# One loop of seven passes on TensorE, with two shared buffers and GpSimd handing out its waits

## The chip, the cores and the metric

The kernel runs on one core of one Trainium2 chip. The metric is the device time of one execution in microseconds (us). Before the change it is 265.19 us, the median of three runs (265.16 to 265.31). A core has five engines that run their own instruction streams and meet only at semaphores: TensorE (PE, with its weight loads listed apart as PEld), VectorE (DVE), ScalarE (ACT), GpSimd (POOL) and SyncE (SP). Here SP does nothing but start transfers from memory. Sixteen DMA engines carry them.

## The reference, cut to what matters

One decode step of a transformer block for 8 sequences: layer norm, attention over the last 1024 positions of a cache, residual, layer norm, gated feed-forward, residual. Everything is float32, and every weight is used once.

```python
W = min(4096, max(256, Sk // 4))                # 1024
q = (layernorm(x) @ wq)                         # 8 x 1024 by 1024 x 4096
scores = einsum(q, k_cache[:, :, Sk - W:]) * (Dh ** -0.5)
o = einsum(softmax(scores), v_cache[:, :, Sk - W:])
h = x + o @ wo                                  # 8 x 4096 by 4096 x 1024
g, u = layernorm(h) @ w_gate, layernorm(h) @ w_up   # 1024 x 3584 each
out = h + (gelu(g) * u) @ w_down                # 3584 x 1024
```

The operands are 16.8 MB each for wq, the keys, the values and wo, and 14.7 MB each for gate, up and down: 111.15 MB that must come from memory.

## The kernel before, in words

**Loads.** SP issues every large transfer in the order of use. There are two buffers of 64 KB a partition (8.39 MB each). `load` (L127) takes them in turn: wq in two halves, keys in two, values in two, wo in two, then gate and up for the first four blocks of 512 columns (`gu0_0`, `gu0_1`). A load waits on SP until PE has marked the last product of what the buffer held before (`free[wb]`). The gate and up of the remaining three blocks (48 KB a partition each), and `w_down` in six parts (`PARTS`, 8, 8, 4, 4, 2 and 1 row blocks of 128 rows) and a last block in two column halves (`ends`), are laid out as a ring over the same 128 KB (L413 to L453). So there is always one load in flight and one or more waiting behind it.

**Side loads.** Of row block 19 (`SIDE`) the last 296 columns do not come with their part. Eight small transfers of 4 rows (L440) bring them to a tile of their own, `w_side`, from which eight extra products are made (L476).

**Products.** The 8 tokens are repeated to 32 columns. Each product takes a 128 x 32 stationary tile and 512 columns of the buffer. Four of them write the four groups of 32 PSUM partitions. A load of 8.39 MB is 32 such products; each is two matmul instructions and two weight loads in the stream. Between loads PE transposes what VectorE has made of the last sums (L192), and VectorE or ScalarE copies it into the next stationary tile. Every product of the program is written out: the PE stream is straight-line code.

**The tail.** The pair of row blocks 24 and 25 (L466), a single block (L489), the sum of the four PSUM groups through `d1` (L480 and L489), and the two `ends` halves (L501), two copies to SBUF on ACT (L504) and two output transfers.

## Time and profile before

| what | value |
|---|---|
| median of three runs | 265.19 us |
| span of the profiled execution | 264.1 us |
| outside the span, so median less span | 1.1 us |
| moved by the DMA queues | 111.44 MB, 422 GB/s on the mean |
| PE busy | 142.2 us (54%) |
| DVE, ACT, POOL busy | 23.3, 10.9, 5.5 us |

A row of the timeline gives start, duration, engine, line, operation, `out<-in`, shapes and the count of merged instructions; in brackets stands the idle time before it and what ended that. `x64` for a load's products are the 32 products with two matmul instructions each. A row of the windows view gives a stretch, its length, the busy time of each engine in it, the granted TensorE clock, the mean busy share of the 16 DMA engines and the GB/s moved. In the list of DMA queues `q1` carries what SP issues, `q10` what ACT issues and `q8 instruction` the transfers that refill an engine's instruction memory.

### The profile page before, as it was taken

The numbers are of one execution on the slowest core, as the hardware profiler recorded it, in microseconds if no ns is written. First come the engines' busy times: TensorE is split into PE (matmuls) and PEld (weight loads), VectorE is DVE, ScalarE is ACT, GpSimd is POOL, SyncE is SP. The second block draws the span as 40 slices with busy tenths as digits, with TensorE's granted clock in tenths as the row PEclk, the third lists the DMA queues.
The fourth block names the chain that finished last, engine by engine and source line by source line (L and its number), as shares of the span: only waits on it lengthen the run. The fifth ranks groups of instructions, "written<-read, shape, count | busy, mean of one in ns | idle before, by whom it ended". The sixth has DMA issues, their size and how long they took to land.

```text
span 264.1 us, 2072 instructions
## 1 busy us (share of the span) xinstructions
PE 142.2 (54%) x958; PEld 40.9 (15%) x958; DVE 23.3 (9%) x55; ACT 10.9 (4%) x17; POOL 5.5 (2%) x15
## 2 busy tenths in 40 slices
PE   0006905905905906907807507818609477589875
PEld 0002201201201301302202102212102111113122
DVE  0040000000020110110110100170000200000001
ACT  1020000000010020020000000020000000000000
POOL 8000000000000000000000000000000000000000
PEclk9999985865875975985956965975957959599999
DMA  8998999999899989999998999899998999999994
GB/s 318 481 437 357 476 476 390 407 466 466 347 466 466 459 347 466 459 407 417 447 466 367 469 437 466 377 447 457 429 419 387 476 402 427 417 462 409 410 413 181
DMA packets 3256, 111.44 MB, mean 422 GB/s; under 512 B 392, under 2 KB 648, under 8 KB 1072
## 3 DMA queue, kind: packets, MB, share of 16 engines
q1 hardware_dynamic: 3088, 111.22, 97.9%
q8 instruction: 7, 0.11, 0.2%
q10 hardware_dynamic: 160, 0.10, 0.1%
q14 instruction: 1, 0.01, 0.0%
HBM read 111.18 MB, written 0.13 MB: 421 GB/s over the span
## 4 chain that ended last, share of the span: by engine, by line
DMA 78%; PE 21%; SPq 0%; issue 0%; ACT 0%
DMA w<-gu 20%; DMA w<-wq 16%; DMA w<-v 11%; DMA w<-kt 11%; DMA w<-wo 11%; DMA w<-dn 9%; PE big L380 6%; PE tb L312 4%; PE tb L237 4%; PE ya L340 3%; PE big L265 3%; SPq L91 0%; PE acc L489 0%; ACT o_fin L504 0%; PE tb L489 0%
## 5 line engine op out<-in xcount | busy, mean ns | idle before, releaser
L380 PE MATMUL big<-w,ln_t 128*32 128x512 f32 x224 | 37.7, 752 | 19.8 <-DMA w<-gu 19.8
L265 PE MATMUL big<-w,qz 128*32 128x512 f32 x128 | 18.8, 753 | 18.3 <-DMA w<-kt 18.3
L340 PE MATMUL ya<-w,ot 128*32 128x512 f32 x128 | 17.9, 721 | 19.9 <-DMA w<-wo 19.9
L466 PE MATMUL ya<-w,at 128*32 128x512 f32 (+1 forms) x104 | 16.4, 591 | 3.2 <-DMA w<-dn 3.2
L380 PEld LDWEIGHTS big<-w,ln_t 128*32 128x32 f32 x224 | 9.2, 134 | 46.9 <-issue 24.9
L192 PE MATMUL ta<-ident,ln_xn 64*128 64x64 f32 x16 | 2.2, 318 | 24.4 <-DVE ln_xn L218 24.4
L312 PE MATMUL tb<-w,pt 128*32 128x512 f32 x64 | 9.9, 787 | 9.0 <-DMA w<-v 9.0
L312 PE MATMUL acc<-w,pt 128*32 128x512 f32 x64 | 9.4, 751 | 9.5 <-DMA w<-v 9.5
L237 PE MATMUL tb<-w,ln_t 128*32 128x512 f32 x64 | 9.8, 783 | 8.6 <-DMA w<-wq 8.6
L237 PE MATMUL acc<-w,ln_t 128*32 128x512 f32 x64 | 9.2, 742 | 2.6 <-DMA w<-wq 2.6
L340 PEld LDWEIGHTS ya<-w,ot 128*32 128x32 f32 x128 | 4.8, 128 | 31.5 <-issue 31.5
L265 PEld LDWEIGHTS big<-w,qz 128*32 128x32 f32 x128 | 4.8, 134 | 31.6 <-issue 22.5
L466 PEld LDWEIGHTS ya<-w,at 128*32 128x32 f32 x104 | 4.2, 109 | 15.0 <-issue 10.6
L393 DVE TENSOR_TENSOR hm<-ge,big 128x512 f32<-128x512 f32 (+1 forms) x2 | 1.4, 684 | 56.6 <-PE big L380 56.6
L192 PEld LDWEIGHTS ta<-ident,ln_xn 64*128 64x128 f32 x16 | 1.8, 216 | 25.3 <-DVE ln_xn L218 25.3
L274 DVE TENSOR_REDUCE nmax<-big 128x1 f32<-128x1024 f32 x2 | 2.4, 1224 | 33.8 <-PE big L265 33.8
L276 ACT ACTIVATE p<-big,nmax 128x1024 f32<-128x1024 f32 x2 | 2.2, 1113 | 71.9 <-DVE nmax L274 71.9
L312 PEld LDWEIGHTS tb<-w,pt 128*32 128x32 f32 x64 | 2.6, 139 | 15.6 <-issue 15.6
L312 PEld LDWEIGHTS acc<-w,pt 128*32 128x32 f32 x64 | 2.5, 135 | 15.7 <-issue 15.7
L237 PEld LDWEIGHTS tb<-w,ln_t 128*32 128x32 f32 x64 | 2.3, 139 | 15.4 <-DMA w<-wq 8.8
L237 PEld LDWEIGHTS acc<-w,ln_t 128*32 128x32 f32 x64 | 2.5, 134 | 8.6 <-issue 8.6
L209 ACT ACTIVATE ln_sd<-ln_ve 64x1 f32<-64x1 f32 x2 | 0.4, 203 | 73.9 <-DVE ln_ve L208 73.9
(81 smaller groups left out, 53.1 us busy)
## 6 DMA issues: line engine op xcount, KB each, us to landing
w<-gu SPq DMA_DIRECT2D x2, 6144.0 KB, 23.9
w<-dn SPq DMA_DIRECT2D x2, 4096.0 KB, 27.0
w<-dn SPq DMA_DIRECT2D x1, 2048.0 KB, 19.6
w<-dn SPq DMA_DIRECT2D x1, 1900.0 KB, 23.3
w<-dn SPq DMA_DIRECT2D x1, 1024.0 KB, 21.7
w<-dn SPq DMA_DIRECT2D x1, 512.0 KB, 22.5
w<-ends SPq DMA_DIRECT2D x2, 256.0 KB, 22.7
w_side<-side SPq DMA_DIRECT2D x8, 18.5 KB
```

The source lines that it names most:

```text
L192: tok = run("tensor", lambda e, i=i: e.transpose(t[:, i, :], src[:, i * P:(i + 1) * P], ident[:rows, :rows]), id_ok, ready, clear, mark=(i ...
L209: tok = run("scalar", lambda e: e.activation(sd, ve, AF.Sqrt), tok)
L237: tok = run("tensor", lambda e, c=c, j=j: e.matmul(q_ps[32 * j:32 * j + 32, :], xt[c], w[:, c, j * N:(j + 1) * N], start=(c == 0), stop=(c ...
L265: tok = run("tensor", lambda e: e.matmul(s_ps[32 * r:32 * r + 32, k0:k0 + N], qz[hf][:, s, c0:c0 + 32], k_t[:, s, half * HB + b, k0:k0 + N ...
L274: tok = run("vector", lambda e: e.tensor_reduce(out=nmax, in_=s_ps, axis=AX.X, op=ALU.max, negate=True), tok)
L276: p_ok = run("scalar", lambda e: e.activation(p_sb, s_ps, AF.Exp, bias=nmax, accum_out=tot), tok)
L312: tok = run("tensor", lambda e: e.matmul(o3[32 * r:32 * r + 32], pt[:, c, 32 * r:32 * r + 32], v_t[:, s, c, half * HB:(half + 1) * HB, :], ...
L340: tok = run("tensor", lambda e: e.matmul(ya[32 * r:32 * r + 32, :], ot[:, 2 * hf * REP + h + e2].rearrange("p r b -> p (r b)"), w[:, h + e ...
L380: tok = run("tensor", lambda e: e.matmul(pair[32 * j:32 * j + 32, s, :], ht[c], w[:, c, j * N:(j + 1) * N], start=(c == 0), stop=(c == NC ...
L393: tok = run("vector", lambda e: e.tensor_mul(hm[:rows], ge[:rows], pair[:rows, 1, :]), tok, g_ok)
L466: tok = run("tensor", lambda e: e.matmul(ya[32 * r:32 * r + 32, 0:n], at[:, q + e2, :], rows_of(q + e2)[:, ch * N:ch * N + n], start=(r no ...
```

## The change

All products are brought to one form, and PE runs them in a loop.

* **Two buffers, two stationary tiles, two PSUM pairs.** `buf[0]`, `st[0]`, `ob[0]` serve the first half of a pass (`a`), `buf[1]`, `st[1]`, `ob[1]` the second (`b`). A half is 8 steps of 4 products; the first 4 steps sum in one PSUM bank, the last 4 in the other, so the two banks are added afterwards by VectorE. Passes 0 to 5 are q, scores, values, wo, gate and up (blocks 0 to 3), gate and up (blocks 4 to 6, with 8 early row blocks of `w_down` in the free quarter of the load). Pass 6 has a first half alone: 16 row blocks of `w_down`.
* **Loads.** 11 transfers of 8.39 MB (`w_k_s`), the twelfth in two halves, pass 6 in 4, 2 and 2 steps (`wd0` to `wd2`), then a pair (`wp`), a single (`ws`) and the two `ends`. The side loads are gone; the input `x` comes in one transfer and not in two.
* **Waits.** PE waits on one semaphore, `go`, each time for 1, and takes it down again. GpSimd, after its own constants, walks a list in PE's order, waits for whatever each place needs and raises `go`.
* **The loop.** `Fori` over 7 passes on PE alone, with a branch that skips the second half in the last pass and one that runs the residual's products (`fold`, `res`) in pass 3 alone. Each transposition takes 8 blocks of 128 x 128, whether 1, 4 or 8 are used.
* **Tail.** After the loop: pair, single, `d1`, ends as before, with `d1` now the sum of two banks and of `d0`, which holds the residual and the early rows' sums.

```diff
-SET = NQ * N
-PARTS = (8, 8, 4, 4, 2, 1)
-SIDE = 19
+STEPS = 8
+LOAD = STEPS * NQ * N
+PASSES = 7
+WO, GU0, GU1, DN = 3, 4, 5, 6
+CUTS = (0, 4, 6, STEPS)
...
+    landed = {(0, 0): [move("w_0_0", buf[0], w[0])]}
+    x_in = move("x", x_sb[0:ROWS:STEP, :], x, x_zero, engine="scalar")
+    landed[0, 1] = [move("w_0_1", buf[1], w[1])]
+    for k in range(1, DN):
+        for s in range(2):
+            n = 2 * k + s
+            free = pe(f"{'ab'[s]}{k - 1}")
+            if (k, s) == (GU1, 1):
+                half = LOAD // 2
+                landed[k, s] = [
+                    move(f"w_{k}_{s}_{i}", buf[s][:, i * half:(i + 1) * half], w[n + i], free)
+                    for i in range(2)]
+            else:
+                landed[k, s] = [move(f"w_{k}_{s}", buf[s], w[n], free)]
+    landed[DN, 0] = [
+        move(f"wd{i}", buf[0][:, a * NQ * N:b * NQ * N], dn[i], pe(f"a{GU1}"))
+        for i, (a, b) in enumerate(zip(CUTS, CUTS[1:]))]
+    w_pair = buf[1][:, 0:NQ * N]
+    pair_in = move("wp", w_pair, pair, pe(f"b{GU1}"))
...
+    def tokens_in(ready):
+        xt = t8[:, :, 0:ROWS].rearrange("p n (b s) -> p n b s", s=STEP)[:, :, :, 0]
+        a = run("vector", lambda e: e.tensor_copy(
+            st[0].rearrange("p (c r b) -> p c r b", c=NC, b=B),
+            xt.unsqueeze(2).to_broadcast([P, NC, P // B, B])), *ready)
+        b = run("scalar", lambda e: e.copy(st[1], st[0]), a)
+        return a, b
...
-            side_in = fl.sem("w_side")
-            for h, src in enumerate(side):
-                p0 = h % 4 + 32 * (h // 4)
-                fl.start("sync", lambda e: e.dma_start(w_side[p0:p0 + 13:4], src), [zero[-1]]).then_inc(
-                    side_in, 16)
...
+    tok = run("vector", lambda e: e.tensor_add(d1, ob[0][:, 0:N], d0), pe(f"a{DN}h"), d0_ok, ex_ok)
...
+    d1_ok = run("vector", lambda e: e.tensor_add(d1, ob[0][:, N:2 * N], d1), pair_done, tok)
...
+    for name in pe_waits():
+        left = fl.missing("gpsimd", need.pop(name, []))
+        for s, v in left[:-1]:
+            nc.gpsimd.wait_ge(s, v)
+        if left:
+            nc.gpsimd.wait_ge(*left[-1]).then_inc(go, 1)
+        else:
+            nc.gpsimd.sem_inc(go, 1)
...
+    def wait():
+        nc.tensor.wait_ge(go, 1).then_inc(go, -1)
...
+    def turn(src):
+        for i in range(NC):
+            ins = nc.tensor.transpose(t8[:, i, :], src[:, i * P:(i + 1) * P], ident)
+        marked(ins)
+
+    def products(s, cuts):
+        for i in range(STEPS):
+            if i in cuts:
+                wait()
+            for r in range(NQ):
+                c = i // (STEPS // 2) * N
+                ins = nc.tensor.matmul(
+                    ob[s][32 * r:32 * r + 32, c:c + N], st[s][:, i * P + 32 * r:i * P + 32 * r + 32],
+                    buf[s][:, (i * NQ + r) * N:(i * NQ + r + 1) * N],
+                    start=(i % (STEPS // 2) == 0), stop=(i % (STEPS // 2) == STEPS // 2 - 1))
+            if i % (STEPS // 2) == STEPS // 2 - 1:
+                marked(ins)
+
+    wait()
+    turn(xs[1])
+    with nc.Fori(0, PASSES, engines=[mybir.EngineType.PE]) as it:
+        products(0, CUTS)
+        with nc.tensor.If(it < DN):
+            wait()
+            turn(xs[0])
+            products(1, (0, STEPS // 2))
+            with nc.tensor.If(it == WO):
+                wait()
+                for ch in range(2):
+                    ins = nc.tensor.matmul(
+                        fin[0:ROWS, ch * N:(ch + 1) * N], to_rows[:, ch, :], y_sb, start=True, stop=True)
+                marked(ins)
...
+            wait()
+            turn(xs[1])
```

What this moves on PE, at the start of the program. Before, each stage has rows of its own (`ln_t`, `qz`, `pt` are the stationary tiles of q, scores and values):

```order
L192 MATMUL ta<-ident,ln_xn 128x64 x8
L237 MATMUL acc<-w,ln_t 32x512 x32
L192 MATMUL ta<-ident,q 128x128 x4
L237 MATMUL tb<-w,ln_t 32x512 x32
L192 MATMUL ta<-ident,q 128x128 x4
L265 MATMUL big<-w,qz 32x512 x64
L192 MATMUL ta<-ident,p 128x128 x4
L192 MATMUL ya<-ident,p 128x128 x4
L312 MATMUL acc<-w,pt 32x512 x32
```

After, one body stands for all stages; the branches are instructions of PE (behind these rows come the loop's counter and its branch back):

```order
L433 MATMUL tt<-ident,xs 128x128 x8
L451 UNCONDITIONAL_BRANCH
L442 MATMUL o<-w,st 32x512 x32
L453 COMPARE_AND_BRANCH
L433 MATMUL tt<-ident,xs 128x128 x8
L442 MATMUL o<-w,st 32x512 x32
L457 COMPARE_AND_BRANCH
L460 MATMUL fin<-y_sb,to_rows 64x512 x2
L465 MATMUL fin<-h_sb,spread 32x512 x2
L457 UNCONDITIONAL_BRANCH
L433 MATMUL tt<-ident,xs 128x128 x8
L453 UNCONDITIONAL_BRANCH
```

The products of six stages have become two rows of 32 that are run again and again, and after each of them stand 8 transpositions where there were 1, 4 or 8.

On SP, from the gate and up loads to the end, before:

```order
L91 DMA w<-gu 128x16384 x2
L91 DMA w<-gu 128x12288 x2
L91 DMA w<-dn 128x8192 x2
L440 DMA w_side<-side 4x1184 x8
L91 DMA w<-dn 128x3800
L91 DMA w<-dn 128x4096
L91 DMA w<-dn 128x2048
L91 DMA w<-dn 128x1024
L91 DMA w<-ends 128x512 x2
```

and the whole of SP's transfers after (`w<-ends` are all pieces that are cut from one array, from the twelfth load's halves on):

```order
L81 DMA w<-w 128x16384 x11
L81 DMA w<-ends 128x8192 x3
L81 DMA w<-ends 128x4096 x2
L81 DMA w<-ends 128x2048
L81 DMA w<-ends 128x1024
L81 DMA w<-ends 128x512 x2
L81 DMA out<-o_fin 128x128
```

The eight transfers of 4 rows have gone, every load now spans all 128 partitions, and the last four loads are of the same sizes as before.

## The prediction

> **What bounds the kernel now.** I read the page first, then PE's timeline, then the DMA list cut at the landings, then the windows at the end.

> ```profile
> span 264.1 us, 2072 instructions
> PE 142.2 (54%) x958; PEld 40.9 (15%) x958; DVE 23.3 (9%) x55; ACT 10.9 (4%) x17; POOL 5.5 (2%) x15
> q1 hardware_dynamic: 3088, 111.22, 97.9%
> q8 instruction: 7, 0.11, 0.2%
> DMA 78%; PE 21%; SPq 0%; issue 0%; ACT 0%
> ```

> The 16 DMA engines are busy 97.9% of the span with the kernel's own 111.2 MB, and the chain of waits is 78% transfers. PE's 21% there are products between a landing and the issue of the load that replaces it. PE's timeline shows that this costs the stream nothing; the loads' first products, in order:

> ```profile
> 23.17 9.22 PE L237 MATMUL acc<-w,ln_t 128*32 128x512 f32 x64 [2.64 <-DMA w<-wq]
> 42.43 9.83 PE L237 MATMUL tb<-w,ln_t 128*32 128x512 f32 x64 [8.57 <-DMA w<-wq]
> 62.56 10.01 PE L265 MATMUL big<-w,qz 128*32 128x512 f32 x64 [8.82 <-DMA w<-kt]
> 82.02 8.82 PE L265 MATMUL big<-w,qz 128*32 128x512 f32 x64 [9.45 <-DMA w<-kt]
> 101.40 9.36 PE L312 MATMUL acc<-w,pt 128*32 128x512 f32 x64 [9.54 <-DMA w<-v]
> 120.81 9.89 PE L312 MATMUL tb<-w,pt 128*32 128x512 f32 x64 [9.02 <-DMA w<-v]
> 140.21 8.74 PE L340 MATMUL ya<-w,ot 128*32 128x512 f32 x64 [9.25 <-DMA w<-wo]
> 159.84 9.16 PE L340 MATMUL ya<-w,ot 128*32 128x512 f32 x64 [10.64 <-DMA w<-wo]
> 179.19 9.72 PE L380 MATMUL big<-w,ln_t 128*32 128x512 f32 x64 [1.30 <-DMA w<-gu]
> 198.45 8.63 PE L380 MATMUL big<-w,ln_t 128*32 128x512 f32 x64 [9.55 <-DMA w<-gu]
> ```

> A load lands about every 19.4 us and PE is done with it after 9 to 10, so the next load for that buffer is queued more than 9 us before the DMA engines run out of work. Only the stream and what follows its last byte set the time.

> The periods are not equal. From the starts: 19.26, **20.13**, 19.46, 19.38, 19.41, 19.40, **19.63**, 19.35, 19.26. The DMA list, cut from 23.2 to 42.4 us and from 42.4 to 62.5, tells what is special in the long one:

> ```profile
> DMA packets 144, 8.39 MB, mean 437 GB/s; under 512 B 16, under 2 KB 16, under 8 KB 16
> DMA packets 145, 8.41 MB, mean 418 GB/s; under 512 B 16, under 2 KB 16, under 8 KB 16
> q8 instruction: 1, 0.02, 0.3%
> ```

> The long period has one packet more, 16 KB of PE's instructions (0.11 MB over 7). A load has landed only when the last of 16 engines is done, and one such packet made the last engine 0.75 us later (20.13 less the mean of the other seven normal periods, 19.36). The second long period, +0.27, holds one too (the same list from 140.1 to 159.7 counts one), and others fell in normal periods: they hit engines that were not the last. If all seven had hit one engine, the landings would have slid by 7 x 0.75 = 5.3 us; they slid by about 1. So each delayed another engine. The end shows the result:

> ```profile
> 258.60:259.20 0.60, 0.06 (x4) 0.06 (x8) 0.00 (x0) 0.00 (x0) 0.00 (x0) 1.00 0.97 382
> 259.20:259.80 0.60, 0.60 (x8) 0.09 (x8) 0.00 (x0) 0.00 (x0) 0.00 (x0) 1.00 0.68 263
> 259.80:260.40 0.60, 0.42 (x8) 0.02 (x4) 0.13 (x1) 0.00 (x0) 0.00 (x0) 1.00 0.72 277
> 260.40:261.00 0.60, 0.60 (x16) 0.35 (x16) 0.56 (x1) 0.00 (x0) 0.00 (x0) 1.00 0.32 123
> 261.00:261.70 0.70, 0.70 (x29) 0.65 (x29) 0.06 (x1) 0.00 (x0) 0.00 (x0) 1.00 0.01 3
> ```

> The DMA share (next to last column) falls over nearly 2 us: some engines are done at 259.2, others at 261. The mean engine ends at 259.2 + 0.6 x (0.68 + 0.72 + 0.32) = 260.2, 0.8 before the last.

> **The change part by part.**

> *The instruction stream (the main term).* The page counts 958 matmul instructions and 958 weight loads, 1916, and 7 refills: one for each 256 to 274 instructions. In the change the program text holds, by the rows of PE's order, 96 products and 24 transpositions, that is 96 x 2 + 24 = 216 matmul instructions, 432 with their weight loads: less than two refills' worth. The loop's body is 68 products and 16 transpositions, 304 instructions: more than one refill holds, less than two. If what is in instruction memory stays, the seven refills go. By the rate: the stream ran from the second landing (42.4) to the last. The row of the last pieces gives that one:

> ```profile
> L91 SPq DMA_DIRECT2D w<-ends x2: 431/432/432, 238.3 to 238.8; - x2
> DMA to landing us min/median/max: 22.6/22.7/22.8
> ```

> 238.8 + 22.8 = 261.6. In these 219.2 us came 111.15 - 16.78 = 94.4 MB. At a normal period's rate (8.39 MB in 19.36 us, 433 GB/s) they need 217.8: 1.4 us less. That is an upper bound, as the small pieces at the end may never reach the full rate. By the engines: 0.8 us of imbalance, plus the refills' own time, 0.2% of 264.1 = 0.5 us an engine, less the imbalance that stays because the engines don't start together. I can't read the latter off a row; between 0 and 0.8 the gain is 0.5 to 1.3. Between 0.5 and 1.4 I take **1.1**: two normal neighbours, 19.26 and 19.46, differ by 0.2, so the engines' order at the start seems to matter little.

> *Side loads removed.* Eight times 18.5 KB go and w_down's part grows from 1900 KB to 2048: the same bytes, spread over all engines instead of shifted to some. **0** (in the 1.1, which assumes an even spread).

> *The form of the loads.* 8.39 MB as before, and the last four pieces have the same sizes as before. **0.**

> *More work between passes.* All transpositions are now 8 of 128 x 128, the stationary tile is 128 x 1024, and each sum has two banks to add.

> ```profile
> L192 PE MATMUL ta<-ident,q 128*128 128x128 f32 x8 | 1.3, 286 | 1.6 <-DVE q L243 1.6
> L223 DVE COPY ln_t<-ta 128x256 f32<-128x256 f32 x2 | 0.8, 424 | 2.4 <-PE ta L192 2.4
> L354 DVE TENSOR_TENSOR h_sb<-x_sb,big 64x1024 f32<-64x1024 f32 x1 | 1.2, 1214 | 2.2 <-PE big L351 2.2
> L393 DVE TENSOR_TENSOR hm<-ge,big 128x512 f32<-128x512 f32 x1 | 0.7, 686 | 28.9 <-PE big L380 28.9
> ```

> Eight transpositions took 1.3 us, four of them half: +0.65. An extra sum is +0.7, a copy to 128 x 1024 about 1.2 instead of 0.4. So a change of pass grows by 2 to 3 us, under covers of 8.6 to 9.6 us of idle PE (the brackets above). The one thin cover is 1.30 us, at 179.19, where residual and layer norm stand ahead of gate and up. There the additions are the copy (+0.8), transpositions (1.3 against 1.1) and the hand-overs: up to 1.5 us, so PE may start 0.2 late. Late next is the issue of the load that reuses the buffer, and it has over 9 us. **0.** Without that cover it would cost 2 to 3 us in each of 12 halves.

> *GpSimd between PE and what it waits for.* No row has this hand-over. Behind GpSimd's waiting instruction are only later waits in PE's order. The nearest is a hand-over from ACT to DVE in the layer norm:

> ```profile
> 17.52 0.20 ACT L209 ACTIVATE ln_sd<-ln_ve 64x1 f32<-64x1 f32 x1 [12.70 <-DVE ln_ve L208]
> 17.76 0.15 DVE L210 RECIPROCAL ln_r<-ln_sd 64x1 f32<-64x1 f32 x1 [0.27 <-ACT ln_sd L209]
> ```

> ACT ended at 17.72, DVE began at 17.76: a hop is under 0.1. There are now two hops instead of one; bounds 0 and 0.3 a wait. All are under the same covers but for the last, `wd2`'s, and the pieces behind it are waited for by PE itself:

> ```profile
> 256.64 1.92 PE L466 MATMUL ya<-w,at 128*32 128x512 f32 x16 [0.93 <-DMA w<-dn]
> 259.14 1.07 PE L466 MATMUL ya<-w,at 128*32 128x512 f32 x8 [0.57 <-DMA w<-dn]
> 260.38 0.43 PE L489 MATMUL acc<-w,at 128*32 128x128 f32 x8 [0.17 <-DMA w<-dn]
> 261.70 0.40 PE L501 MATMUL tb<-w,at 128*32 128x128 f32 x8
> 261.95 0.27 ACT L504 COPY o_fin<-acc 128x128 f32<-128x128 f32 x1 [22.45 <-PE acc L501]
> ```

> 0.57 us of idle PE covers it. **0**, at most 0.3.

> *The tail.* After the pair (landed 259.1): 4 products, one VectorE instruction of 0.7, eight small products, the ends, ACT, the transfer out. The same instructions in the same order; `d1` is an addition instead of a copy (686 against 691 ns). It moves with the landings. The loop's two branches stand ahead of the pair under the same 0.57 us. **0**, bounds 0 and 0.5.

> Sum: 264.1 - 1.1 = 263.0 of span; with the 1.1 us around it, or from the median, 265.2 - 1.1 = **264.1 us**.

> [...]

> **The rivals.**

> 1. *The loop refetches in every pass (slower).* Place: the branch back, from the body's second piece to its first. For it: PE took a refill at each piece of straight code, and the body needs two pieces. Against: nothing in the trace shows a piece dropped that is still wanted. PE's own stall would lie under the 9 us covers; the price is the engines'. One refill delays an engine by at least 0.75 and, by the width of the end, at most 1.8; I take 1.5. It decides from the point where some engine is hit twice, the 17th refill at the latest. With 13 refills (first piece back, next piece ahead) on different engines, all end about 1.5 late: 264.1 + 1.5 = 265.6, no change. With three a pass, 19, some engines are hit twice: 264.1 + 3 = 267.1 at most. All on one engine would be 10 us, which the slide in the trace speaks against.

> 2. *One to three refills remain (no change).* The second piece has to come in once. For it: the first refill in the trace came at the first piece's end. One engine is 1.5 late: 264.1 + 0.4 to 1.5, centre 264.9.

> 3. *The tail takes it back.* The pair's products wait for the loop's exit longer than 0.57 us: 264.1 + 0.5 to 1.

> 4. *PE is late for a buffer.* It would need 9 us more in a half; ruled out to a few per cent.

> **How the numbers follow.** About 0.2% (0.53 us) is what a measurement can tell from no change, so the limits are 264.66 and 265.72. Forecast 0.43 (263.7 to 264.5; 0.41 faster, 0.02 within). Rival 1: 0.28, of which 0.08 within (up to 16 refills) and 0.20 above, to 267.1 and a little beyond. Rival 2: 0.17 (264.5 to 265.8; 0.03 faster, 0.12 within, 0.02 slower). Rival 3: 0.06 (0.01, 0.02, 0.03). Rival 4, with whatever else a rewrite of this size can bring, 0.06, slower. Together faster **0.45**, within **0.24**, slower **0.31**. The range, 263.6 to 266.6, leaves out about half of rival 1's upper part, rival 4 and the edges: 2 in 10. The forecast's own is 263.7 to 264.5.

> **What would show it.** Right: no `q8 instruction` row, or one packet; all periods 19.3 to 19.4; the DMA share at the end falling within 1 us; products beginning within 0.1 us of each landing except in pass 4. Wrong: a `q8` row with 13 or more; periods that grow; PE idle for "issue" before the pair's products; a second thin cover in another pass.

## The result: 0.5% slower, and no longer the same from run to run

The changed kernel takes **266.66 us** (median of 11 runs, 265.39 to 267.86) against 265.22 (11 runs, 265.08 to 265.46): ratio 1.0047, interval 1.0032 to 1.0061. Forecast were 264.1 us, in a range of 263.6 to 266.6, and a gain. Before, the runs lay within 0.4 us; now within 2.5, four of them at 265.4 to 265.6, seven from 266.6 up.

The page after, two lines of its head and three queues (packets, MB, share):

```profile
span 265.4 us, 2321 instructions
PE 139.6 (53%) x1000; PEld 47.7 (18%) x1000; DVE 39.9 (15%) x84; ACT 18.3 (7%) x27; POOL 5.5 (2%) x15
q1 hardware_dynamic: 3024, 111.22, 97.5%
q8 instruction: 2, 0.03, 0.1%
q14 instruction: 2, 0.02, 0.0%
```

PE's refills went from 7 to 2, as the change's mechanism wants; one of the two falls into the stream (48.57 us), the other at its end (263.05). The two packets of 8 KB on q14 fall into the stream as well, at 169.96 and 250.48 us; before had one, at 262.25, behind the stream. The page doesn't say which engines they serve. VectorE's counted instructions went from 55 to 84 and ScalarE's from 17 to 27, and in e6 below, with fewer instructions on GpSimd, one of the two packets is gone. The stream moves the same bytes. The first products of a load into the first buffer, or into the second (42.36, 82.21, 198.43), in PE's timeline, without the transpositions between them:

```profile
23.00 9.54 PE L442 MATMUL o<-w,st 128*32 128x512 f32 x64 [6.44 <-PEq L426]
42.36 8.40 PE L442 MATMUL o<-w,st 128*32 128x512 f32 x64 [7.74 <-PEq L426]
62.87 8.39 PE L442 MATMUL o<-w,st 128*32 128x512 f32 x64 [10.02 <-PEq L426]
82.21 8.95 PE L442 MATMUL o<-w,st 128*32 128x512 f32 x64 [7.18 <-PEq L426]
101.56 9.51 PE L442 MATMUL o<-w,st 128*32 128x512 f32 x64 [6.63 <-PEq L426]
...
182.71 9.90 PE L442 MATMUL o<-w,st 128*32 128x512 f32 x64 [1.48 <-PEq L426]
198.43 7.05 PE L442 MATMUL o<-w,st 128*32 128x512 f32 x48 [4.80 <-PEq L426]
```

The periods are 19.36, **20.51**, 19.34, 19.35: the long one is still there, in the same place as the 20.13 before. The list of transfers from 42.2 to 62.5 us has the reason, one refill:

```profile
DMA packets 145, 8.41 MB, mean 414 GB/s; under 512 B 16, under 2 KB 16, under 8 KB 16
q8 instruction: 1, 0.02, 0.3%
```

The last two pieces of w_down, by the rows of their tile (issue of the first and the last, then the time to landing):

```profile
L81 SPq DMA_DIRECT2D w<-ends x2: 431/432/432, 244.6 to 245.1; - x2
DMA to landing us min/median/max: 16.3/16.4/16.4
```

245.1 + 16.4 = 261.5 us; before it was 261.6. So the stream ends where it ended, and the loss lies behind it. PE's timeline at the end:

```profile
246.94 3.64 PE L442 MATMUL o<-w,st 128*32 128x512 f32 x32 [0.46 <-PEq L426]
251.82 1.92 PE L442 MATMUL o<-w,st 128*32 128x512 f32 x16 [1.24 <-PEq L426]
256.72 3.59 PE L442 MATMUL o<-w,st 128*32 128x512 f32 x16 [2.98 <-PEq L426]
260.11 1.06 PE L476 MATMUL o<-w,at 128*32 128x512 f32 x8
260.98 0.62 PE L485 MATMUL fin<-w,at 128*32 128x128 f32 x16
262.05 0.64 PE L485 MATMUL fin<-d,add 128*32 128x128 f32 x16 [0.45 <-DVE mark L398]
262.51 0.62 PE L494 MATMUL fin<-w,at 128*32 128x128 f32 x16
```

The 2 MB piece at 251.82 takes 1.92 us, the next one, of the same size, 3.59. The pair begins at 260.11 instead of 259.14, without any idle time ahead of it, and PE's last product ends at 263.13 instead of 262.10. The windows say why (columns as before; the third from the right is the granted clock):

```profile
253.30:256.70 3.40, 0.44 (x6) 0.01 (x1) 0.00 (x0) 0.00 (x0) 0.00 (x0) 1.00 1.00 419
256.70:260.10 3.40, 3.38 (x16) 0.91 (x20) 0.00 (x0) 0.00 (x0) 0.00 (x0) 0.50 0.91 357
```

PE was busy for 0.44 of 3.4 us, and in the next 3.4 us its granted clock was 0.50 and not 1.00, exactly while the last big products ran. In the kernel before, two things filled this place:

```profile
251.83 2.77 PE L466 MATMUL ya<-w,at 128*32 128x512 f32 x16 [1.24 <-DMA w<-dn]
254.53 1.19 PE L476 MATMUL ya<-w_side,at_side 48*32 48x296 f32 x8
```

The second row is the side products. The first is row blocks 16 to 19, as at 251.82 in the new kernel, but it takes 2.77 us instead of 1.92: in the kernel before, the products of row blocks 16 and 17 (listed in `SLOW`) write two of the four PSUM groups and not all four. The change dropped this arrangement too. Where the old tail had a gap of 0.93 us, the new one has 2.98.

### The profile page after: what moved, and what is told of

Same layout as the page of the kernel before. It is cut to its first block, busy times and chain, and to the rows that moved or that the text cites. A ratio compares the mean times of both kernels' runs of the same rounds, so it can differ in the third digit from the quotient of the medians.

```text
span 265.4 us, 2321 instructions
## 1 busy us (share of the span) xinstructions
PE 139.6 (53%) x1000; PEld 47.7 (18%) x1000; DVE 39.9 (15%) x84; ACT 18.3 (7%) x27; POOL 5.5 (2%) x15
## 3 DMA queue, kind: packets, MB, share of 16 engines
q1 hardware_dynamic: 3024, 111.22, 97.5%
## 5 line engine op out<-in xcount | busy, mean ns | idle before, releaser
L442 PE MATMUL o<-w,st 128*32 128x512 f32 x832 | 118.9, 732 | 87.0 <-PEq L426 79.1
L442 PEld LDWEIGHTS o<-w,st 128*32 128x32 f32 x832 | 32.9, 131 | 163.5 <-issue 163.5
L433 PE MATMUL tt<-ident,xs 128*128 128x128 f32 x104 | 15.7, 300 | 33.6 <-PEq L426 33.6
L433 PEld LDWEIGHTS tt<-ident,xs 128*128 128x128 f32 x104 | 12.6, 153 | 44.3 <-issue 44.3
L272 DVE TENSOR_REDUCE nmax<-o 128x1 f32<-128x1024 f32 x2 | 2.4, 1224 | 33.2 <-PE o L442 33.2
L298 DVE SCALAR_TENSOR_TENSOR xs<-o,share,xs 128x128 f32<-128x128 f32 x14 | 4.9, 351 | 4.3 <-PE o L442 3.8
L274 ACT ACTIVATE xs<-o,nmax 128x1024 f32<-128x1024 f32 x2 | 2.2, 1114 | 40.1 <-DVE nmax L272 40.1
L295 DVE TENSOR_SCALAR xs<-o,share 128x128 f32<-128x128 f32 x2 | 0.7, 352 | 22.7 <-PE o L442 22.7
L354 ACT COPY g<-o 128x512 f32<-128x512 f32 x2 | 1.2, 586 | 35.4 <-PE o L442 35.4
L363 DVE TENSOR_TENSOR u<-ge,o 128x512 f32<-128x512 f32 x2 | 1.4, 687 | 14.0 <-PE o L442 14.0
L364 DVE TENSOR_TENSOR u<-ge,o 128x512 f32<-128x512 f32 x2 | 1.4, 688 | 13.8 <-PE o L442 13.8
L235 DVE COPY st<-tt 128x1024 f32<-128x1024 f32 x2 | 2.4, 1224 | 4.4 <-PE tt L433 4.4
L305 DVE COPY st<-tt 128x512 f32<-128x512 f32 x4 | 2.6, 686 | 2.6 <-PE tt L433 2.6
L327 ACT COPY d<-fin 32x512 f32<-32x512 f32 x1 | 0.6, 574 | 28.3 <-PE fin L465 28.3
## 6 DMA issues: line engine op xcount, KB each, us to landing
w<-ends SPq DMA_DIRECT2D x2, 256.0 KB, 16.4
```

What stands on the lines that cost most here:

```text
L235: a = run("vector", lambda e: e.tensor_copy(st[0].rearrange("p (c r b) -> p c r b", c=NC, b=B), xt.unsqueeze(2).to_broadcast([P, NC, P // ...
L272: tok = run("vector", lambda e: e.tensor_reduce(out=nmax, in_=ob[s], axis=AX.X, op=ALU.max, negate=True), pe(f"{h}1"))
L274: tok = run("scalar", lambda e: e.activation(xs[s], ob[s], AF.Exp, bias=nmax, accum_out=tot), tok)
L298: tok = run("vector", lambda e: e.scalar_tensor_tensor(out, o3[:, b], sh[:, b:b + 1], out, op0=ALU.mult, op1=ALU.add), tok, ready)
L305: tok = run("vector", lambda e: e.tensor_copy(heads[:, g], turned.unsqueeze(2).to_broadcast([P, REP, P // 2 // B, B])), pe(f"t{h}2"))
L433: ins = nc.tensor.transpose(t8[:, i, :], src[:, i * P:(i + 1) * P], ident)
```

## The experiments

Times are medians with their range and the number of runs; the kernel before, run beside them, stayed at 265.24 to 265.28. The last landing is that of the profiled execution.

| label | edit | us | ratio, interval | span | last landing |
|---|---|---|---|---|---|
| e1_cuts | last 2 MB piece waited for in two halves | 266.73 (266.20-267.52, 6) | 1.0053, 1.0039-1.0068 | 265.5 | 261.7 |
| e2_dummy | 8 unread products ahead of the third piece | 266.35 (265.26-267.61, 12) | 1.0043, 1.0027-1.0060 | 264.8 | 261.8 |
| e3_unroll | the seven passes written out | 266.60 (265.72-267.53, 7) | 1.0042, 1.0024-1.0060 | 265.3 | 261.7 |
| e4_noside | kernel before without side loads | 265.85 (265.36-266.51, 12) | 1.0026, 1.0016-1.0035 | 264.4 | 261.9 |
| e5_dense | gaps of the tail filled, too far | 267.10 (266.91-267.42, 5) | 1.0070, 1.0057-1.0083 | 265.6 | 261.5 |
| e6_dense_merge | the same, fewer instructions on GpSimd | 267.07 (267.00-267.25, 5) | 1.0068, 1.0055-1.0081 | 265.7 | 261.6 |
| e7_noside_dense | e4 with its gaps filled, too far | 266.16 (265.93-266.99, 6) | 1.0037, 1.0025-1.0049 | 264.6 | 261.5 |
| e8_fill | gaps filled with room left | **265.59 (265.31-265.83, 11)** | 1.0013, 1.0004-1.0022 | 264.1 | 261.4 |
| e9_again | the changed kernel once more | 265.59 (one run) | - | 264.3 | 261.6 |
| e10_again | the changed kernel a third time | 265.59 (one run) | - | 264.3 | 261.6 |
| e11_unroll_fill | e8 with the passes written out | 265.72 (265.54-265.83, 11) | 1.0016, 1.0007-1.0025 | 264.2 | 261.6 |
| e12_noside_fill | e4 filled with room left | 265.50 (265.32-265.89, 11) | 1.0013, 1.0004-1.0021 | 264.2 | 261.7 |

**e1_cuts: is it the length of one gap?** The last of the three waits is split, so that the longest gap is 1.4 us.

```diff
-CUTS = (0, 4, 6, STEPS)
+CUTS = (0, 4, 6, 7, STEPS)
```

> The changed kernel with the second 2 MB piece of pass 6 cut into two of 1 MB (wd2, wd3), so that PE's longest idle time in the tail falls from 2.98 us to about 1.5. Theory A (clock): after 2.98 us of idle the granted clock falls to 0.5 and the last 8 products take 3.59 us instead of 1.92, 1.0 us of which reaches the end; which executions are hit depends on how the idle time falls against the clock's steps, hence 265.4 to 267.9. Expected: clock 1.00 in the whole tail, median 265.2 to 265.6, all runs within 0.5 us. Theory B (refills): the spread comes from which DMA engines the instruction refills hit; then the median stays at 266.4 to 266.9 and the spread at 2.5 us. Theory C (loop exit): the branches hold PE up; no change either.

No gain: 266.73. PE's timeline of this kernel:

```profile
254.36 1.06 PE L443 MATMUL o<-w,st 128*32 128x512 f32 x8 [0.56 <-PEq L427]
256.85 1.07 PE L443 MATMUL o<-w,st 128*32 128x512 f32 x8 [1.42 <-PEq L427]
259.31 1.93 PE L477 MATMUL o<-w,at 128*32 128x512 f32 x8 [1.39 <-DMA w<-ends]
```

and its windows:

```profile
255.30:258.70 3.40, 1.20 (x12) 0.19 (x8) 0.00 (x0) 0.00 (x0) 0.00 (x0) 1.00 0.99 407
258.70:262.10 3.40, 2.79 (x24) 1.06 (x24) 0.69 (x2) 0.00 (x0) 0.00 (x0) 0.50 0.41 152
```

The clock fell all the same, only later, and now it is the pair that takes 1.93 instead of 1.06. With gaps no longer than 1.42 us but only 1.20 us of work in 3.4, the granted clock went to 0.50. So the length of one gap doesn't decide (1.42 us here, 2.98 in the changed kernel); in both traces a stretch of 3.4 us with little work, 1.20 and 0.44 us, stands ahead of the half clock (e9 below has one that doesn't).

**e2_dummy: keep PE at work.** Eight products that nobody reads run ahead of the third wait, in every pass.

```diff
+            if s == 0 and i == 6:
+                for g in range(2 * NQ):
+                    nc.tensor.matmul(fin[...], st[s][...], buf[s][...], start=True, stop=True)
             if i in cuts:
                 wait()
```

> The changed kernel with 8 products more in the first half of each pass, ahead of the wait for the last piece, written to a PSUM bank that nobody reads then (useless work; the output is the reference's). Transfers are untouched; the idle time ahead of the last piece falls from 2.98 to about 1.1 us. Theory A (clock): as in the run with finer pieces, 265.2 to 265.6, narrow. Theories B and C: as the changed kernel, 266.4 to 266.9, or later, since PE has more to do.

The profiled execution has the full clock and its last products take 1.93 us, but the median of 266.35 and the spread of 2.4 us miss the clock theory's 265.2 to 265.6 and lie near those of the changed kernel. The mean granted clock of each run speaks against the clock as the cause of this spread: the six runs with spans from 265.0 us up have 0.814 to 0.821, the six shorter ones 0.806 to 0.820, and one more stretch of 3.4 us at half clock would lower it by 0.006 (an estimate: half of 3.4 us in a span of 265). So something else seems to lengthen runs of this kernel. In the traced execution a refill of PE's instructions stands at 262.38 us, beside the transfer out, which takes 2.0 us from issue to landing (1.6 in e9, which has no such refill). What the long runs looked like no trace shows.

**e3_unroll: the loop alone undone.** `nc.Fori` and `nc.tensor.If` become Python's `for` and `if`; nothing else changes.

> The changed kernel with its seven passes written out, so that PE's stream is straight-line again; all else as in the change. Refill count back to about 7 or 8. Theory R (what the prediction priced: each refill delays one DMA engine by about 1.5 us, the slowest of 16 sets the landing): with one refill left in the loop the slowest engine was already 1.3 us late at the end, with seven it is 1.5 to 2.0, so last landing 261.7 to 262.3 against 261.55, time 0 to 0.6 us above the changed kernel. Theory L (the loop itself costs: branches, pages brought in again): 0.5 us or more below the changed kernel. Clock theory: the tail's idle time is unchanged, so the spread of over 2 us stays.

Its queue of instructions, and its timeline at the third piece:

```profile
q8 instruction: 8, 0.13, 0.2%
```

```profile
256.91 3.54 PE L442 MATMUL o<-w,st 128*32 128x512 f32 x16 [3.02 <-PEq L426]
```

Eight refills instead of two, and the time is that of the loop, as far as runs that spread over 1.8 us can tell. The half-clock tail (0.50 from 256.8 to 260.2 us) is there without a loop, so neither the loop's branches nor its fewer refills make it.

**e4_noside: what the side loads were worth.** In the kernel before, w_down's row block 19 is loaded whole.

```diff
-SIDE = 19
+SIDE = -1
```

> The kernel before, without the side loads: row block 19 comes whole with its part, the eight products from the side tile are gone. PE is then idle for about 2.9 us ahead of the 2 MB part that follows (254.5 or earlier to 256.6). Theory A (clock): in some executions the clock falls to 0.5 there; 265.2 to 267.0 with a spread of over 1 us. Price 0 for the side loads (the prediction): 265.2, narrow. Theory S (the side loads balance the engines that the refills delay): the last landing 0.3 to 0.5 us later, 265.5 to 265.8, narrow.

0.58 us, not 0: the first hint that the prediction's zero for them was wrong. The gap ahead of the next part is 2.04 us and not 2.9, since the part with row blocks 16 and 17 still takes 2.77 us. The median and the spread of 1.15 us are those of theory A, but in the profiled execution the 16 records at 256.82 us take 1.92 us, the time at full clock, so it doesn't show a half clock in the tail. The last landing is 0.25 us later, a little less than theory S wanted.

**e5_dense, e6_dense_merge, e7_noside_dense: all gaps filled.** 12 unread products ahead of the last transpositions, 8 ahead of the second 2 MB piece, 18 ahead of the third and 4 ahead of the pair; in e6 GpSimd's empty releases are joined as well; in e7 the kernel of e4 gets 8, 10 and 4 ahead of the last three.

```diff
+            if s == 0 and i in (4, 6):
+                with nc.tensor.If(it == DN):
+                    for g in range(8 if i == 4 else 18):
+                        nc.tensor.matmul(fin[...], st[s][...], buf[s][...], start=True, stop=True)
             if i in cuts:
                 wait()
```

> The changed kernel with products that nobody reads put into every gap of its tail, in the last pass alone: 12 ahead of the last transposes, 8 ahead of the second 2 MB piece, 18 ahead of the third, 4 ahead of the pair. Theory (the clock gate makes the loss and the spread: PE is busy for under half of some 3.4 us step near the end, the next step runs at half clock, and whether it falls on the last products depends on where the steps begin): the profile shows clock 1.0 from about 241 us to the end, the last 16 records at 1.9 us instead of 3.59, a span of 264.0 to 264.8, a median of 265.2 to 265.7 and no run above 266.2. Rival (the spread is the DMA engines', or that of the hand-over): median 266.3 to 266.8 as for the changed kernel, with runs above 267, though the profiled clock is 1.0.

> The kernel of e5_dense with GpSimd's releases that need no wait of their own joined to the one before (fewer instructions on GpSimd). Theory: the 8 KB refill on q14 that lands near 250 us in the changed kernel is GpSimd's and goes, and the time does not move unless that refill sits on the engine that is last: within 0.3 us of e5_dense. Rival (these refills carry a good part of the loss): 0.5 us or more below e5_dense, 264.7 or less.

> The kernel before without its side loads and side products, with products that nobody reads in the gaps that they leave (8, 10 and 4 ahead of the last three pieces). Theory (the side products were worth the clock that they kept up): the 0.6 us that their removal cost comes back, median 265.1 to 265.4, highest run below 265.8. Rival (the side loads balance the 16 engines): stays at 265.7 to 266.0, with runs above 266.3.

e5 and e7 missed, and by my own sizing; e6 lies within 0.3 us of e5, as expected. In e5's timeline the fill runs past the landing:

```profile
253.69 4.06 PE L442 MATMUL fin<-w,st 128*32 128x512 f32 x34
257.16 0.62 PE L449 MATMUL o<-w,st 128*32 128x512 f32 x2
```

A product is two records and 16 records take 1.92 us, so 18 products are over 4 us in a gap of 3. But one thing is new: with PE at work throughout, five runs lie within 0.5 us. e6 lost one of the two q14 packets and no time; as PE set the end there, it says nothing about what the packet costs elsewhere. (e7's longest run, 266.99 us, has a span of 264.6 as the others; its excess lies outside the span.)

**e8_fill, e9_again, e10_again: the fill sized by the gaps, and two more executions of the changed kernel.** The edit of e5 with 4 products ahead of the last transpositions, 4 ahead of the second and 8 ahead of the third piece, none ahead of the pair.

> e5_dense was filled too far: a product takes 0.23 us, its 18 ahead of the third piece 4.1 us in a gap of 3.0, and the real ones ran late (257.6 instead of 256.7), so that PE set the end at a full clock. Here the fill is 4 products ahead of the last transposes, 4 ahead of the second 2 MB piece (0.9 us in a gap of 1.2), 8 ahead of the third (1.9 in 3.0), in the last pass alone. Clock theory: clock 1.0 to the end, last products at 256.7 for 1.9 us, span 264.0 to 264.6, median 265.1 to 265.7, no run above 266.3. Rival (the spread is not the clock's): median 266.2 or more with runs above 267, as e2_dummy.

> The changed kernel once more, for another execution's trace. Clock theory: where the granted clock is 1.0 from 256.5 us to the last product, those 16 records take 1.9 us and the span is 264.1 to 264.5; where a half-clock step of 3.4 us begins between 255 and 258.5 us, they take 2.5 to 3.6 us and the span is 265 to 266.5; the last landing is 261.5 to 261.9 in both. Rival (the transfers make the spread): the span follows the last landing instead.

> The changed kernel a third time, with the expectation of e9_again: the span goes with the clock of the last products (264.1 to 264.5 at 1.0, 265 to 266.5 with a step at 0.5), not with the last landing (261.5 to 261.9).

These settle the clock theory for the executions that were traced. e8 is at 265.59 in 11 runs that lie within 0.5 us. Its end in PE's timeline:

```profile
253.44 1.93 PE L442 MATMUL fin<-w,st 128*32 128x512 f32 x16
256.60 1.92 PE L449 MATMUL o<-w,st 128*32 128x512 f32 x16 [1.24 <-PEq L426]
259.04 1.06 PE L489 MATMUL o<-w,at 128*32 128x512 f32 x8 [0.52 <-DMA w<-ends]
```

And the changed kernel itself, in the execution of e9, first the timeline:

```profile
256.78 1.92 PE L442 MATMUL o<-w,st 128*32 128x512 f32 x16 [3.01 <-PEq L426]
259.23 1.06 PE L476 MATMUL o<-w,at 128*32 128x512 f32 x8 [0.52 <-DMA w<-ends]
```

and the windows:

```profile
251.90:255.30 3.40, 1.87 (x16) 0.41 (x16) 0.00 (x0) 0.00 (x0) 0.00 (x0) 1.00 0.98 417
255.30:258.70 3.40, 1.92 (x16) 0.50 (x16) 0.00 (x0) 0.00 (x0) 0.00 (x0) 1.00 1.00 405
```

The same program, the same gap of 3 us, the same last landing, and a clock of 1.00 in both stretches, with 1.87 and 1.92 us of work in them. In the execution shown first the half clock lasted from 256.71 to 260.13 us, and the 3.41 us ahead of it held 0.44 us of work. The same place in e9, 253.30 to 256.70, holds 0.47 us, and behind it the clock is 1.00. So little work in 3.4 us doesn't decide by itself either. My estimate is that the clock is set at borders 3.4 us apart and that they fall by chance: in the first execution one stretch between them held nearly the whole gap, and in e9 they would lie 1.4 us earlier (251.90 against 253.30), so that two stretches share it. No change of the clock in e9's tail shows them. e10 is like e9 (the records at 256.79 take 1.93 us, clock 1.00). The span goes with the clock (265.4 at half, 264.3 at full), not with the landing (261.55, 261.59 and 261.63). Of the 1.1 us between them 0.9 is the later end of PE's products (263.13 against 262.25) and the rest the transfer out (below).

One reservation remains on e8. The fill also makes PE's program longer, and with that its refills move: to 31.62 and 261.44 us, and the second one is over before the packets of the transfer out move. e2, whose trace has the late refill and a full clock, spreads over 2.4 us, and e8 over 0.5. No run moves the refill alone, so what the clock costs is shown in the traced executions, and its share in the medians is not shown apart.

**e11_unroll_fill, e12_noside_fill: the loop, and the side loads, at a full clock.** e8 with Python's `for` and `if` in the place of the loop; e4 with 4 unread products ahead of each of the last two 2 MB pieces.

> e8_fill with its seven passes written out: the loop alone is undone, at a full clock in the tail. The one or two instruction refills of PE become eight. Prediction's main term (refills cost 1.1 us): median 266.5 to 266.9, last landing 262.5 or later. Theory from the landings so far (the mean landing moves 0.2 to 0.5 us, the last one not at all, since the other engines run on while one is held): within 0.3 us of e8_fill, 265.4 to 265.9, last landing 261.4 to 261.9.

> The kernel before without side loads and side products (265.85 us, 265.36 to 266.51), with 4 products that nobody reads ahead of the 2 MB pieces (0.9 us in gaps of 1.3 and 2.0); e7_noside_dense put in 8, 10 and 4 and ran late, as e5_dense. Theory (the side products' worth was the clock): median 265.1 to 265.5, highest run below 265.9. Rival (the side loads balance the engines): 265.7 to 266.0, runs above 266.2.

e11 has eight refills (`q8` reads as in e3), e8 two: 265.72 and 265.59. One refill of each falls at the very end of the stream, at 261.4 us, so seven stand against one within it. The loop is worth 0.13 us (0.10 against the kernel before beside each), which the intervals of the two don't tell from nothing. e12 gets back 0.35 of the 0.58 us that the side loads' removal had cost. 0.23 remains, and in e8 0.35: what that is stays open. The balance of the engines is one candidate (the last landing of e12 is 0.13 us after that of before); it wasn't tried by itself.

None of these beats the kernel before; e8 comes nearest among those with the loop.

## Why the prediction was wrong

*The main term, 1.1 us for the refills.* The mechanism was right: five of seven went, and no piece was fetched again. Rival 1, with 13 refills or more, is out: the page has 2. What failed is the step "Between 0.5 and 1.4 I take **1.1**", a price for all seven together. The text before it had said that each refill delays another engine, and that a load has landed when the last of 16 is done. From the two it follows that the first refill costs what the seventh does not: with one engine 1 us behind, six more engines can be behind as well. The one long period, 20.51 us with its one refill, slides the stream by 1.15; the two long ones of before, with seven refills, by 0.77 (0.75 in the prediction, which is a slip) + 0.27 = 1.04. The one refill that is left would not go by the prediction's own count, since the body's 304 instructions need more than one piece of 256 to 274; no traced run was without it. e11 against e8 measures the step from seven to one: 0.13 us, not 1.1. Their landings say the same. In e8 one period is 20.66 us and the others 19.34 to 19.36; in e11 the periods of 20.31, 19.41 and 19.56 stand out from the same 19.35. The slide is 1.3 us with one refill and 1.2 with seven. This was rival 2, held at 0.17; its 264.9 was 0.7 below e8.

*The end of the stream.* "If all seven had hit one engine ... So each delayed another engine" was right; the mean engine's end, "0.8 before the last", was then read as if the last would come down to the mean. e8 and e11 differ in the loop alone. The windows at the end, e8's (two refills):

```profile
259.20:259.80 0.60, 0.60 (x8) 0.00 (x0) 0.00 (x0) 0.00 (x0) 0.00 (x0) 1.00 0.58 212
259.80:260.40 0.60, 0.40 (x8) 0.12 (x8) 0.16 (x1) 0.00 (x0) 0.00 (x0) 1.00 0.19 72
260.40:261.00 0.60, 0.57 (x19) 0.30 (x18) 0.53 (x2) 0.00 (x0) 0.00 (x0) 1.00 0.06 24
261.00:261.70 0.70, 0.70 (x28) 0.70 (x32) 0.00 (x0) 0.00 (x0) 0.00 (x0) 1.00 0.09 23
```

and e11's (eight):

```profile
259.20:259.80 0.60, 0.60 (x8) 0.14 (x8) 0.00 (x0) 0.00 (x0) 0.00 (x0) 1.00 0.78 297
259.80:260.40 0.60, 0.45 (x7) 0.00 (x0) 0.02 (x1) 0.00 (x0) 0.00 (x0) 1.00 0.58 222
260.40:261.00 0.60, 0.54 (x16) 0.41 (x16) 0.60 (x1) 0.00 (x0) 0.00 (x0) 1.00 0.45 174
261.00:261.70 0.70, 0.68 (x26) 0.58 (x25) 0.07 (x2) 0.00 (x0) 0.00 (x0) 1.00 0.11 32
```

In the next to last column nearly half of e11's engines are at work after 260.4, in e8 one of 16 (0.06). The last one is at work after 261.0 in both. Taking refills away made fewer engines late; it made the last one hardly less late. In the 16 landing events of the last piece the mean engine of e11 is at 260.79 and that of e8 at 260.21, the last at 261.60 and 261.43. After 260.7 stand 9 events in e11, which has 7 refills of PE and 2 packets of q14 in its stream, and 3 in e8, which has 1 and 2; so each of them delayed another engine.

*Side loads, 0.* Wrong, and a step that turned the sign: their bytes were weighed, their products not. The row `254.53 1.19 ... w_side` is in PE's timeline of before, in the middle of what is the long gap of the new tail. Taking the side loads out cost 0.58 us in the kernel before (e4); the fill of e12 brings back 0.35 of it. The prediction gives no term at all to row blocks 16 and 17, whose products kept PE busy for 0.85 us more in the same place; no run undid this alone.

*The tail, "The same instructions in the same order ... It moves with the landings", 0 to 0.5.* The landings stayed and the pair moved by 0.97. Every duration had been taken from a tail at full clock, in rows that showed the clock column at 1.00, without asking what keeps it there. From the changed kernel to e8, whose edit is the fill alone, the median falls by 1.07 us: three quarters of the 1.44 lost (with the reservation on e8's refills above). In the profiled execution a smaller part came on top, the transfer out. Its row in the changed kernel's list of transfers:

```profile
out<-o_fin SPq DMA_DIRECT2D x1, 64.0 KB, 1.9
```

and in e9's:

```profile
out<-o_fin SPq DMA_DIRECT2D x1, 64.0 KB, 1.6
```

The changed kernel's second refill runs beside it (263.05 us), e9's trace has none there: 0.3 us.

*The rest.* GpSimd's hand-over cost what was allowed: the products at 42.36 begin 0.2 after the landing (under 0.1 before). In pass 4 PE was to start 0.2 us late; it started 3.8 late (182.71; the load was in at 178.9), because residual, layer norm, transpositions and widening follow one another there. More than half of it is ScalarE's: the layer norm's activation begins at 177.24, 2.1 us after its input (175.14), behind two copies of the residual's sums (L327 and L328, 0.57 and 0.58 us) and a table load (1.28 us); in the kernel before it followed its input at once (174.88). The prediction's list of added work has neither. The cover that was named held: the next half began at 198.43, on time. Rival 3 named the right place and the wrong cause: PE doesn't wait at the loop's exit.

## What to carry to other kernels

A load is in with the last of its 16 landing events (the changed kernel's second load at 42.19 us, its products from 42.36), and stalls on different DMA engines didn't add up here: the stream slid by 1.2 us with seven refills and by 1.3 with one, and the times differ by 0.13 us (e11 against e8). Ask how late the last engine is, not how many stalls there are. Before taking small work off TensorE near the end of a kernel, add up its busy time over every stretch of 3.4 us there, in any position. Here a stretch with 0.44 us stood ahead of the half clock in the changed kernel, where 16 records then took 3.59 us and not 1.92, and one with 1.20 us in e1; with 0.47 us in e9 the clock stayed full. A few products that nobody reads, sized to leave the landing free, left the clock at 1.00 here (e8, 253.3 to 263.5 us); one gap filled in every pass (e2) was not enough to make the runs short. When the runs of a kernel spread where they did not before, profile more than one execution.

## What the runs showed of the hardware

A refill of PE's instructions is one packet of 16 KB that takes 1.0 to 1.2 us (1.03 to 1.16 over the 9 of the kernel before and the changed kernel); by the landing events above, those of e11 and e8 came on a different engine each. The two packets of q14 in the changed kernel's stream are of 8 KB and take 0.31 us each. By the last piece's landing events the last engine is 1.6 us behind the first in e8, with one refill in the stream, and 1.7 in e11, with seven.

Open are the 0.2 to 0.4 us between e8 or e12 and the kernel before, and why all six runs of e1 are long (266.20 us and more). Open are also e2's long runs and those of the changed kernel above 267 us: no trace of such a run was taken.
